# K of a cached-attention kernel loaded in four partition-interleaved transfers per pack instead of two

## The chip, the cores and the metric

The kernel runs on one core of a Trainium2 chip. The time is device microseconds from start to end of one execution. Each core has five engines that run their own instruction streams: TensorE (PE; its weight loads are shown as PEld), VectorE (DVE), ScalarE (ACT), GpSimd (POOL) and SyncE (SP, which here only issues DMAs). Sixteen DMA engines move data between HBM and the on-chip memory SBUF; matmul results go to PSUM.

## What is computed

Two independent attention blocks, A and B, of the same shapes, whose outputs are set side by side:

```python
B, Sq, D = 16, 64, 640          # x: [B, Sq, D]
H, Sk, Dh = 32, 512, 128        # k_cache, v_cache: [B, H, Sk, Dh]
q = (x @ wq).reshape(B, Sq, H, Dh).transpose(0, 2, 1, 3)
scores = einsum("bhqd,bhkd->bhqk", q, k_cache) * Dh ** -0.5
p = softmax(scores)
o = einsum("bhqk,bhkd->bhqd", p, v_cache)
block = o.transpose(0, 2, 1, 3).reshape(B, Sq, H * Dh) @ wo
out = concatenate([block_A, block_B], axis=-1)
```

All tensors are bfloat16. The caches are the bulk of the data: K and V of both blocks are 268 MB of the 295 MB that the profile shows moved.

## The kernel before

**Packs.** The work is cut into 128 packs. A pack is two batches times four heads: its K and its V are 1 MB each. Four consecutive packs (j = 0 to 3, 16 heads) share the same two batches, eight such groups make a phase (16 heads of all batches), and there are four phases (two blocks, two halves of the heads). The weights for a phase are loaded during the phase before.

**Steps of a pack n**, by the names in the code and the lines of the profile:
- LDK (`em_LDK`, L542 to L548): two DMAs of 512 KB, one for each batch b, of 64 rows of 8 KB (32 keys of 128 values). The rows of batch b go to every second partition, `kn_ring[b::2]`. The ring has 6 slots.
- LDV (`em_LDV`, L550 to L562): two DMAs of 512 KB, in rows of 4 KB for j = 0 to 2 and in two pieces of 2 KB for j = 3. The ring has 4 slots.
- QP (L598, PE) and QE (L604, ACT): project the queries and copy them out of PSUM.
- KT (`em_KT`, L608 to L613, DVE): two block transposes. Each takes 1024 elements per partition, read as 4-byte words (two bfloat16), and transposes them in blocks of 32 by 32 from `kn_ring` to `kt_ring`. The two batches lie interleaved on the partitions, so the 32 words of a transposed row belong to the two batches in turn; they are written apart by batch (`p c b k`), 16 words each.
- S (L622, PE): scores, 32 matmuls into four PSUM banks.
- EX (L641, ACT): exponentials with row sums; RC (L654, DVE): reciprocals; NM (L670, POOL): normalise.
- TR (L681, PE) transposes the probabilities, TE (L691, DVE) copies them out of PSUM in two instructions, PV (L705, PE) multiplies by V.
- OE, ZO (L713, L717, ACT) copy the result out and zero a bank; OP (L725, PE) multiplies by the output projection; after four packs OS (L735, L738, DVE) takes the sum, and for the second half of the heads ST (L744, ACT's queue) stores it.

**Order.** The order on every engine is written by a planner (`build_plan`). Each step has a time in units of packs (`Cfg.AT`), and each engine runs its steps in the order of those times. PE interleaves packs: PV(n-2), S(n), TR(n-1), OP(n-2), QP(n+1), PV(n-1). DVE: RC(n+1), KT(n+2) twice, TE(n) twice. SP issues all K, V, x and most weight loads in one fixed order, sorted by an issue time that the planner gives (K of a pack about 2.5 packs ahead of its V). Before each step the planner puts the semaphore waits that its data and buffers need: V of pack n waits for PV of pack n-4, K of pack n for the scores of pack n-6.

**Semaphores of loads.** K has one semaphore for each slot and batch, so KT waits for two. V has one for each slot, which both its DMAs raise; `wait_count` rounds a wait on it up to the full pair, and `Clocks.finish` joins what the two DMAs know.

Of the kernel before, what the change touches and what calls it, by code (L numbers as in the profile page):

```python
# [6 lines left out]
F32 = mybir.dt.float32  # L7
# [5 lines left out]
ENGINES = ("sp", "pe", "act", "dve", "pool")  # L13
SUM_MIN = 2.0 ** -40
SUM_MAX = 2.0 ** 40


class Cfg:
    NK = 6
# [11 lines left out]
    AT = dict(XT=-2.485, XE=-2.28, XC=-0.9, QP=-0.45, QE=-0.24, KT=(-1.24, -1.0), S=0,  # L31
              EX=(0.21, 0.32, 0.43, 0.54), RC=(0.53, 0.75), NM=(0.56, 0.69, 0.82, 0.95), NMZ=(0.54, 0.55, 0.56, 0.76), TR=1.2,
              TE=(1.26, 1.39), PV=1.75, OE=(2.0, 2.06), ZO=2.11, OP=2.31, OS=2.545, LDWO=2.6, ST=3.374, WP0=-1.75, WP1=-1.6)
# [22 lines left out]
def build_plan(dims, cfg, general):  # L56
# [7 lines left out]
    AT = cfg.AT  # L64
    ops = []
    loads = []
    at = {}

    def add(eng, kind, idx, ts, reads=(), writes=()):
        op = Op(eng, kind, idx, ts, reads, writes)  # L70
        ops.append(op)
        at[(kind, idx)] = op
        return op

    def add_output(n):
        g, j = n // NJ, n % NJ
        final = n >= 0 and dims["FINAL"](g // NBP)
        for b in range(2):
            tv = n + AT["PV"]
            op = add("sp", "LDV", (n, b), tv - 0.3, [], [("v" if n >= 0 else "absent", n % cfg.NV, b)])  # L80
            loads.append((n - cfg.NV + AT["PV"] + 0.2 if n >= 0 else -99.0, 3, op))
        if n > -2:
            add("pe", "TR", n, n + AT["TR"], [("pn", i) for i in range(4)] + [("ident",)], [("B", 4), ("B", 5)])
        for b in range(2):
            add("dve", "TE", (n, b), n + AT["TE"][b], [], [("B", 4 + b), ("pT", b)])
        add("pe", "PV", n, n + AT["PV"], [("pT", 0), ("pT", 1), ("v", n % cfg.NV, 0), ("v", n % cfg.NV, 1)],
            [("B", 4), ("B", 5), ("B67",)])
        add("act", "OE", (n, 1), n + AT["OE"][0], [], [("B67",), ("oT", 1)])
        add("act", "OE", (n, 0), n + AT["OE"][1], [], [("B", 4), ("B", 5), ("oT", 0)])
        add("act", "ZO", n, n + AT["ZO"], [("zeros",)], [("B67",)])  # L90
        add("pe", "OP", n, n + AT["OP"], [("oT", 0), ("oT", 1), ("wo", j)], [("B67",)])
        if j == NJ - 1:
            bp = g % NBP
            add("dve", "OS", g, n + AT["OS"], [("acc", bp)], [("B67",), ("out_sb",) if final else ("acc", bp)])
            if final:
                add("act", "ST", g, n + AT["ST"], [("out_sb",)], [("out_dram", g)])
# [4 lines left out]
    for g in range(N // NJ + 1):  # L101
# [5 lines left out]
        if dims["FIRST"](g // NBP):  # L107
            add("act", "XE", g, n0 + AT["XE"], [], [("SB", 0), ("xs", g % NBP)])
            op = add("sp", "LDX", g, txt - 0.5, [], [("xn", g % cfg.NXN)])
            loads.append((txt - 3.7 if g else -7.0, 0, op))  # L110
        add("pool", "XC", g, n0 + AT["XC"], [("xs", g % NBP)], [("xT", g % cfg.NX)])
    for ph in range(NPH):
        twp = [ph * PH + j + (AT["WP1"] if ph else AT["WP0"]) for j in range(NJ)]
        for kt in range(dims["KT"] if ph else 0):
            ready = twp[-1] - PH + 0.5 if ph > 1 else NJ - 1 + AT["WP0"] + 0.5
            op = add("sp", "LDWQ", (ph, kt), twp[0] - 0.5, [], [("ws", kt, j) for j in range(NJ)])
            loads.append((ready + 0.5 + 0.5 * kt if ph == 1 else ready + 2.0 + 0.14 * PH * kt, 1, op))
        for j in range(NJ):
# [3 lines left out]
            if not ph:  # L122
                op = add("sp", "LDWQ", (0, j), twp[j] - 0.5, [], [("ws", kt, j) for kt in range(dims["KT"])])
# [11 lines left out]
    for n in range(-2, N):  # L135
        add_output(n)
        if n < 0:
            continue
        g, j = n // NJ, n % NJ
        add("pe", "QP", n, n + AT["QP"], [("xT", g % cfg.NX), ("wqp", j)], [("SB", 1)])  # L140
        add("act", "QE", n, n + AT["QE"], [], [("SB", 1), ("qs", n % cfg.NQ)])
        for b in range(2):
            tk = n + AT["KT"][b]
            add("dve", "KT", (n, b), tk, [("kn", n % cfg.NK, 0), ("kn", n % cfg.NK, 1)], [("kt", n % cfg.NKT, b)])
            op = add("sp", "LDK", (n, b), n + AT["KT"][0] - 0.9, [], [("kn", n % cfg.NK, b)])
            loads.append((n - cfg.NV + AT["PV"] + 0.2 - cfg.KLEAD, 2, op))
        add("pe", "S", n, n + AT["S"], [("qs", n % cfg.NQ), ("kt", n % cfg.NKT, 0), ("kt", n % cfg.NKT, 1)],
            [("SB", i) for i in range(4)])
        for i in range(4):
            h = 4 * n + i  # L150
            te = n + AT["EX"][i]
            if general:
                add("dve", "MX", h, te - 0.002, [], [("SB", i), ("negmax", h % 4)])
            add("act", "EX", h, te, [("negmax", h % 4)] if general else [],
                [("SB", i), ("p", h % cfg.NP), ("rs", h)])
            add("pool" if n < N - 1 else "dve", "NM", h, n + (AT["NM"] if n < N - 1 else AT["NMZ"])[i], [("p", h % cfg.NP), ("recip", n % cfg.NR, i // 3)], [("pn", i)])
        for a in range(2):
            add("dve", "RC", (n, a), n + AT["RC"][a], [("rs", 4 * n + i) for i in ((0, 1, 2), (3,))[a]],
                [("recip", n % cfg.NR, a)])
# [156 lines left out]
class Clocks:  # L316
# [15 lines left out]
    def finish(self, eng, op):  # L332
        ck = self.clock[eng]
        self.val[op.sem] = self.val.get(op.sem, 0) + 1
        c2 = dict(ck)
        if op.dma:
            c2[op.sem] = op.count
        else:
            self.own[eng][op.sem] = op.count
            for s2, v2 in self.own[eng].items():  # L340
                if c2.get(s2, 0) < v2:
                    c2[s2] = v2
        if op.sem[0] == "d_v" and op.count % 2 == 0:
            for s2, v2 in self.snap[(op.sem, op.count - 1)].items():
                if c2.get(s2, 0) < v2:
                    c2[s2] = v2
        self.snap[(op.sem, op.count)] = c2


def wait_count(d):  # L350
    return d.count + d.count % 2 if d.sem[0] == "d_v" else d.count


def order_waits(progs, need, base):
    ks = Clocks(base)

    def visit(eng, op):
        want = {}
        for d in need[id(op)]:
            want[d.sem] = max(want.get(d.sem, 0), wait_count(d))  # L360
        if any(ks.val.get(s, 0) < v for s, v in want.items()):
            return False
        ck = ks.clock[eng]
        cand = [(s_, v_) for s_, v_ in want.items() if ck.get(s_, 0) < v_]
        keep = list(cand)
        for w in list(cand):
            for o in keep:
                if o != w and ks.snap[o].get(w[0], 0) >= w[1]:
                    keep.remove(w)
                    break  # L370
        op.waits = keep
        ks.learn(eng, keep)
        ks.finish(eng, op)
        return True

    run_order(progs, visit)
# [46 lines left out]
def mha_kernel(nc, blocks, out, cfg=None):  # L423
    cfg = cfg or Cfg()
# [4 lines left out]
    KT = D // 128  # L429
# [11 lines left out]
    for general in (False, True):  # L441
        dims = dict(NPH=NPH, NBP=NBP, NJ=NJ, KT=KT, FIRST=lambda ph: ph % NSUB == 0,
                    FINAL=lambda ph: ph % NSUB == NSUB - 1)
        plans.append(build_plan(dims, cfg, general))
    NK, NV, NKT, NX, NXN, NQ, NP, NR = (cfg.NK, cfg.NV, cfg.NKT, cfg.NX, cfg.NXN, cfg.NQ, cfg.NP, cfg.NR)

    with contextlib.ExitStack() as es:
        block = es.enter_context(nc.Block())

        def sb(name, shape, dt):  # L450
            return es.enter_context(nc.sbuf_tensor(name, shape, dt))
# [4 lines left out]
        kn_ring = sb("kn_ring", [128, NK, 2, 2048], BF16)  # L456
# [33 lines left out]
        def pack_info(n):  # L490
            g, j = n // NJ, n % NJ
            ph = g // NBP
            return ph // NSUB, g % NBP, j, ph % NSUB * HPH + 4 * j
# [46 lines left out]
            return ins, ins  # L540

        def em_LDK(e, op):  # L542
            n, b = op.idx
            blk, bp, j, h = pack_info(n)
            src = blocks[blk][1][2 * bp + b, h:h + 4].rearrange("h (p t) d -> (h p) (t d)", t=32)
            dst = kn_ring[b::2, n % NK].rearrange("p a c -> p (a c)")
            ins = e.dma_start(dst, src)  # L547
            return ins, ins  # L548

        def em_LDV(e, op):  # L550
# [57 lines left out]
        def em_KT(e, op):  # L608
            n, a = op.idx
            dst = kt_ring[:, n % NKT, 16 * a:16 * a + 16].rearrange("p t j b k two -> p (t j) b (k two)").bitcast(F32)  # L610
            ins = e.transpose(dst.rearrange("p c b k -> p c k b"),  # L611
                              kn_ring[:, n % NK, a, :].bitcast(F32).rearrange("p (c k b) -> p c k b", k=16, b=2))
            return ins, ins  # L613

        def em_S(e, op):
# [133 lines left out]
        def em_FL1(e, op):  # L749
# [3 lines left out]
            e.wait_ge(s_ch, 2)  # L753
            e.tensor_scalar(extreme[:, 2:3], extreme[:, 0:1], SUM_MAX, None, ALU.is_le).then_inc(s_ch, 1)
            e.tensor_scalar(extreme[:, 3:4], extreme[:, 1:2], SUM_MIN, None, ALU.is_ge).then_inc(s_ch, 1)
# [147 lines left out]
```

## Time and profile before

| | |
|---|---|
| median of 10 runs | 753.63 us (751.88 to 755.1) |
| the profiled execution | 754.1 us |
| its span, first to last instruction | 752.4 us |
| granted TensorE clock, mean | 0.981 |
| PE / DVE / ACT / POOL busy | 679.6 / 677.3 / 520.1 / 404.0 us |
| moved by DMA | 295.13 MB, mean 392 GB/s |
| DMA packets | 83421, of these 74736 on SP's queue |
| K load, issue to landing | median 12.6 us (A), 16.5 us (B) |
| V load, issue to landing | median 11.7 us (A), 13.8 us (B) |

A line of a group in the profile reads: line of the kernel, engine, operation, written tile <- read tiles, shapes, count | busy us, mean ns of one | idle time of the engine just before, and what ended it. The slice rows cut the span into 40 equal slices of 18.8 us; a digit is the busy share in tenths. A row of a stage gives, after its length, the busy time of PE, PEld, DVE, ACT and POOL with the number of instructions, then the granted clock, the busy share of the DMA engines and GB/s. A line of waits reads: engine and line that waited <- engine and line that ended the wait: us in total, times, longest us. "SPq" is the issuing queue of SP.

### The profile page before, as it was taken

The numbers are of one execution on the slowest core, as the hardware profiler recorded it, in microseconds if no ns is written. First come the engines' busy times: TensorE is split into PE (matmuls) and PEld (weight loads), VectorE is DVE, ScalarE is ACT, GpSimd is POOL, SyncE is SP. The second block draws the span as 40 slices with busy tenths as digits, with TensorE's granted clock in tenths as the row PEclk, the third lists the DMA queues.
The fourth block names the chain that finished last, engine by engine and source line by source line (L and its number), as shares of the span: only waits on it lengthen the run. The fifth ranks groups of instructions, "written<-read, shape, count | busy, mean of one in ns | idle before, by whom it ended". The sixth has DMA issues, their size and how long they took to land.

```text
span 752.4 us, 57490 instructions
## 1 busy us (share of the span) xinstructions
PE 679.6 (90%) x26518; PEld 530.2 (70%) x26518; DVE 677.3 (90%) x818; ACT 520.1 (69%) x1559; POOL 404.0 (54%) x580
## 2 busy tenths in 40 slices
PE   3669999999999999999988989999998899999995
PEld 2547777777777777777766777777776677777773
DVE  8549999999999999999978899999997899999983
ACT  1437777877777777777756777777776577777772
POOL 5424555464875454645674455455586455545450
PEclk9979999999999999999999999999999999999996
DMA  8999999999999999999999999999999999999950
GB/s 314 399 402 410 411 411 414 411 411 413 408 399 410 416 413 414 412 413 413 413 399 407 410 411 412 410 413 412 412 407 398 411 415 413 412 414 412 406 195 14
DMA packets 83421, 295.13 MB, mean 392 GB/s; under 512 B 9264, under 2 KB 24112, under 8 KB 66992
## 3 DMA queue, kind: packets, MB, share of 16 engines
q1 hardware_dynamic: 74736, 284.20, 94.5%
q10 hardware_dynamic: 8640, 10.49, 3.9%
q14 instruction: 36, 0.29, 0.1%
q8 instruction: 9, 0.15, 0.1%
HBM read 292.03 MB, written 2.62 MB: 392 GB/s over the span
## 4 chain that ended last, share of the span: by engine, by line
DVE 28%; PE 24%; DMA 16%; SPq 12%; POOL 9%; ACT 5%; issue 5%; ACTq 0%; DVEq 0%
DVE kt_ring L611 20%; DMA kn_ring<-in_B_k_cache_dram 11%; POOL pn_sb L670 8%; PE ps L725 6%; PE ps L705 6%; DVE pT_sb L691 6%; SPq L547 5%; PE ps L598 5%; DMA kn_ring<-in_A_k_cache_dram 5%; ACT p_ring L641 5%; PE ps L622 3%; PE ps L681 3%; SPq L560 3%; SPq L558 2%; DVE recip L654 1%
## 5 line engine op out<-in xcount | busy, mean ns | idle before, releaser
L670 POOL TENSOR_SCALAR pn_sb<-p_ring,recip 128x512 bf16<-128x512 bf16 x508 | 341.8, 692 | 318.0 <-DVE recip L654 318.0
L611 DVE STREAM_TRANSPOSE kt_ring<-kn_ring 128x1024 f32<-128x1024 f32 x256 | 478.6, 1947 | 25.2 <-DMA kn_ring<-in_B_k_cache_dram 21.1
L641 ACT ACTIVATE p_ring<-ps 128x512 bf16<-128x512 f32 x512 | 298.7, 598 | 19.0 <-PE ps L622 4.2
L691 DVE COPY pT_sb<-ps 128x1024 bf16<-128x1024 bf16 x258 | 163.3, 675 | 24.4 <-PE ps L681 24.4
L705 PE MATMUL ps<-pT_sb,v_ring 32*128 32x64 bf16 (+1 forms) x14528 | 158.7, 192 | 22.5 <-DVE pT_sb L691 5.9
L725 PE MATMUL ps<-wo_sb,oT_sb 128*128 128x320 bf16 x1040 | 167.6, 305 | 6.4 <-issue 5.4
L598 PE MATMUL ps<-xT_ring,wqp_sb 128*128 128x128 bf16 x2560 | 167.0, 221 | 5.5 <-POOL xT_ring L587 5.5
L705 PEld LDWEIGHTS ps<-pT_sb,v_ring 32*128 32x128 bf16 (+1 forms) x14528 | 144.2, 92 | 37.4 <-issue 28.6
L598 PEld LDWEIGHTS ps<-xT_ring,wqp_sb 128*128 128x128 bf16 x2560 | 158.4, 114 | 12.0 <-issue 5.7
L713 ACT ACTIVATE oT_sb<-ps 128x256 bf16<-128x256 f32 x260 | 85.6, 381 | 107.4 <-PE ps L705 107.4
L604 ACT ACTIVATE qs_ring<-ps 128x512 bf16<-128x512 f32 x128 | 76.5, 597 | 91.8 <-PE ps L598 91.8
L622 PE MATMUL ps<-kt_ring,qs_ring 32*64 32x512 bf16 x4096 | 139.4, 383 | 0.0
L681 PEld LDWEIGHTS ps<-ident,pn_sb 64*128 64x128 bf16 x4128 | 71.1, 95 | 86.6 <-ACT ps L717 59.5
L725 PEld LDWEIGHTS ps<-wo_sb,oT_sb 128*128 128x128 bf16 x1040 | 92.1, 99 | 44.7 <-issue 5.9
L681 PE MATMUL ps<-ident,pn_sb 64*128 64x64 bf16 x4128 | 84.4, 191 | 29.0 <-POOL pn_sb L670 21.8
L641 ACT ACTIVATION_READ_ACCUMULATOR p_ring<-ps 128x1 f32 x512 | 106.0, 207 | 0.0
L622 PEld LDWEIGHTS ps<-kt_ring,qs_ring 32*64 32x64 bf16 x4096 | 53.3, 103 | 28.8 <-issue 1.0
L654 DVE RECIPROCAL recip<-rowsum 128x3 f32<-128x3 f32 (+1 forms) x256 | 39.4, 160 | 13.6 <-ACT p_ring L641 11.2
L717 ACT ACTIVATE ps<-zeros 128x256 f32<-128x256 bf16 x130 | 51.3, 395 | 0.0
L570 POOL COPY wqp_sb<-ws_sb 128x1280 bf16<-128x1280 bf16 x32 | 39.2, 1254 | 7.3 <-DMA ws_sb<-in_A_wq_dram 7.3
L587 POOL COPY xT_ring<-xs_sb 128x640 bf16<-128x640 bf16 x32 | 22.9, 716 | 3.6 <-PE ps L598 3.6
L577 PE MATMUL ps<-ident,xn_ring 128*128 128x128 bf16 x165 | 15.1, 224 | 3.6 <-DMA xn_ring<-in_A_x_dram 3.6
(26 smaller groups left out, 66.2 us busy)
## 6 DMA issues: line engine op xcount, KB each, us to landing
kn_ring<-in_A_k_cache_dram SPq DMA_DIRECT2D x128, 512.0 KB, 12.6
v_ring<-in_A_v_cache_dram SPq DMA_DIRECT2D x128, 512.0 KB, 11.7
kn_ring<-in_B_k_cache_dram SPq DMA_DIRECT2D x128, 512.0 KB, 16.5
v_ring<-in_B_v_cache_dram SPq DMA_DIRECT2D x128, 512.0 KB, 13.8
ws_sb<-in_B_wq_dram SPq DMA_DIRECT2D x10, 512.0 KB, 17.0
wo_sb<-in_B_wo_dram ACTq DMA_DIRECT2D x8, 640.0 KB, 15.3
ws_sb<-in_A_wq_dram SPq DMA_DIRECT2D x4, 640.0 KB, 9.7
wo_sb<-in_A_wo_dram SPq DMA_DIRECT2D x4, 640.0 KB, 13.8
```

Of the source, the lines that this page charges most:

```text
L598: last = e.matmul(ps[:, 1, f * 128:(f + 1) * 128], w[:, kt, f, :], xT_ring[:, xs, kt, :], start=(kt == 0), stop=(kt == KT - 1))
L604: ins = e.activation(qs_ring[:, op.idx % NQ].rearrange("p f b q -> p (f b q)"), ps[:, 1, :], ACTF.Copy, scale=scale)
L611: ins = e.transpose(dst.rearrange("p c b k -> p c k b"), kn_ring[:, n % NK, a, :].bitcast(F32).rearrange("p (c k b) -> p c k b", k=16, b=2))
L622: last = e.matmul(ps[64 * b:64 * b + 64, i, :], qs_ring[rows, n % NQ, f, b, :], kt_ring[rows, n % NKT, :, f // 2, b, :, f % 2], start=(f = ...
L641: ins = e.activation(dst, src, ACTF.Exp, scale=1.0, accum_out=rowsum[:, h:h + 1])
L670: ins = e.tensor_scalar(dst, src, recip[:, h // 4 % NR, i:i + 1], 1.0, ALU.mult, ALU.mult)
L681: last = e.transpose(pt_bank(b)[:, 64 * c:64 * c + 64], pn_sb[rows, c, :], ident[rows, rows], tile_position=(64 * b, 0))
L691: ins = e.tensor_copy(pT_sb[:, b].rearrange("p t q -> p (t q)"), pt_bank(b))
L705: last = e.matmul(ps[:, 4 + i, 64 * b:64 * b + 64], v_ring[rows, n % NV, b, c, :], pT_sb[rows, b, c, :], start=(t == 0 and i < 2), stop=(t ...
L713: ins = e.activation(oT_sb[:, 2 * a:2 * a + 2, :], o_ps[:, 2 * a:2 * a + 2, :], ACTF.Copy)
L717: ins = e.activation(z_ps, zeros[:, :].rearrange("p (s c) -> p s c", s=2), ACTF.Copy)
L725: last = e.matmul(out_ps[:, s, :], oT_sb[:, i, :], wo_sb[:, 4 * j + i, s * NH0:(s + 1) * NH0], start=(j == 0 and i == 0), stop=(j == NJ - ...
```

## The change

K of a pack comes by four DMAs of 256 KB instead of two of 512 KB. The rows stay 8 KB. Of batch b, the even rows (l = 0) and the odd rows (l = 1) are loaded by separate DMAs, each of 32 rows, to every fourth partition: `kn_ring[2 * b + l::4]`. So the partitions carry the batches in pairs (b0, b0, b1, b1, ...) where they carried them in turn (b0, b1, b0, b1, ...), and a transposed row of 32 words has two neighbouring words of a batch in a row. KT reads as before, in order; it writes `p c h b l`, where l, the innermost, steps to the neighbouring word. What `kt_ring` holds in the end, and every step after KT, are unchanged.

The four DMAs raise one semaphore per slot, and KT waits for that one at its full count; `PARTS` generalises for K (four) what was written for V (two).

```diff
+PARTS = dict(d_v=2, d_k=4)
...
+        for i in range(4):
+            op = add("sp", "LDK", (n, i), n + AT["KT"][0] - 0.9, [], [("kn", n % cfg.NK)])
+            loads.append((n - cfg.NV + AT["PV"] + 0.2 - cfg.KLEAD, 2, op))
         for b in range(2):
             tk = n + AT["KT"][b]
-            add("dve", "KT", (n, b), tk, [("kn", n % cfg.NK, 0), ("kn", n % cfg.NK, 1)], [("kt", n % cfg.NKT, b)])
-            op = add("sp", "LDK", (n, b), n + AT["KT"][0] - 0.9, [], [("kn", n % cfg.NK, b)])
-            loads.append((n - cfg.NV + AT["PV"] + 0.2 - cfg.KLEAD, 2, op))
+            add("dve", "KT", (n, b), tk, [("kn", n % cfg.NK)], [("kt", n % cfg.NKT, b)])
...
-        if op.sem[0] == "d_v" and op.count % 2 == 0:
-            for s2, v2 in self.snap[(op.sem, op.count - 1)].items():
+        part = PARTS.get(op.sem[0], 1)
+        for k in range(op.count - 1, (op.count - 1) // part * part, -1):
+            for s2, v2 in self.snap[(op.sem, k)].items():
...
 def wait_count(d):
-    return d.count + d.count % 2 if d.sem[0] == "d_v" else d.count
+    part = PARTS.get(d.sem[0], 1)
+    return -(-d.count // part) * part
...
         def em_LDK(e, op):
-            n, b = op.idx
+            n, b, l = op.idx[0], op.idx[1] // 2, op.idx[1] % 2
             blk, bp, j, h = pack_info(n)
-            src = blocks[blk][1][2 * bp + b, h:h + 4].rearrange("h (p t) d -> (h p) (t d)", t=32)
-            dst = kn_ring[b::2, n % NK].rearrange("p a c -> p (a c)")
-            ins = e.dma_start(dst, src)
+            src = blocks[blk][1][2 * bp + b, h:h + 4].rearrange("h (p l t) d -> l (h p) (t d)", l=2, t=32)[l]
+            ins = e.dma_start(kn_ring[2 * b + l::4, n % NK].rearrange("p a c -> p (a c)"), src)
             return ins, ins
...
         def em_KT(e, op):
             n, a = op.idx
             dst = kt_ring[:, n % NKT, 16 * a:16 * a + 16].rearrange("p t j b k two -> p (t j) b (k two)").bitcast(F32)
-            ins = e.transpose(dst.rearrange("p c b k -> p c k b"),
-                              kn_ring[:, n % NK, a, :].bitcast(F32).rearrange("p (c k b) -> p c k b", k=16, b=2))
+            src = kn_ring[:, n % NK, a, :].bitcast(F32).rearrange("p (c h b l) -> p c h b l", h=8, b=2, l=2)
+            ins = e.transpose(dst.rearrange("p c b (h l) -> p c h b l", h=8, l=2), src)
             return ins, ins
```

## The prediction

> **What bounds the kernel now.** I read the busy row of the DMA engines first, then the idle time of each engine by stage, then who waits for whom, then single packs from the landing times.
>
> The page:
>
> ```profile
> PE   3669999999999999999988989999998899999995
> DVE  8549999999999999999978899999997899999983
> DMA  8999999999999999999999999999999999999950
> GB/s 314 399 402 410 411 411 414 411 411 413 408 399 410 416 413 414 412 413 413 413 399 407 410 411 412 410 413 412 412 407 398 411 415 413 412 414 412 406 195 14
> L611 DVE STREAM_TRANSPOSE kt_ring<-kn_ring 128x1024 f32<-128x1024 f32 x256 | 478.6, 1947 | 25.2 <-DMA kn_ring<-in_B_k_cache_dram 21.1
> ```
>
> The DMA engines are at 9 tenths from the second slice to about 715 us, and 398 to 416 GB/s hardly changes, whatever the other engines do. The stages in numbers (engine times, then clock, DMA share, GB/s):
>
> ```profile
> 60.00:145.00 85.00, 82.18 (x3288) 64.53 (x3286) 82.92 (x101) 65.82 (x198) 45.70 (x68) 1.00 1.03 411
> 515.00:600.00 85.00, 76.27 (x3008) 59.97 (x3014) 75.99 (x94) 58.12 (x176) 51.32 (x71) 1.00 1.03 408
> 645.00:730.00 85.00, 82.64 (x3290) 64.97 (x3288) 82.86 (x102) 63.60 (x194) 45.70 (x68) 1.00 0.95 381
> ```
>
> In two kinds of stage, one with DVE 97% busy and one with 89%, the DMA share is the same 1.03 (above 1 because records of neighbouring packets overlap). So the queue never runs dry before 715 us, and as SP issues in one fixed order, the moment at which each K and V lands is set by the DMA engines alone. The waits say the same (the first two lines from SP's own queue, the third from 600 to 730 us):
>
> ```profile
> SPq L558 <- PE ps L705: 141.9, 61, 6.8
> SPq L560 <- PE ps L705: 73.9, 30, 4.1
> PE ps L681 <- POOL pn_sb L670: 2.0, 6, 0.4
> ```
>
> SP waits for V slots, yet the queue behind it holds some 15 us of transfers (K takes a median 15.8 us from issue to landing). And PE hardly waits for anybody: 2.4 us of the 85 from 645 us on. Three engines are level: DVE, PE and DMA.
>
> What computing adds to the transfers is the end. From landing times and first PV matmuls: K of pack 102 lands at 592.8 us and its transpose starts at 592.9; from there computing falls behind, K of pack 123 waits 1.9 us for its transpose (702.7 to 704.6) and K of pack 127 2.7 us (723.1 to 725.8). V of pack 123 lands at 715.7 us and is used at 720.4, V of 127 at 730.8 and is used at 741.2. After that come 11.2 us of projection, sum and store in which nothing is transposed.
>
> **The transpose.** Price per element from DVE's contiguous 4-byte writes in this trace:
>
> ```profile
> L735 DVE COPY acc<-ps 128x640 f32<-128x640 f32 x17 | 13.5, 797 | 0.1
> L509 DVE MEMSET v_ring<- 128x4096 uint32 x1 | 3.5, 3472 | 1.7 <-PEq L888 1.7
> L517 DVE MEMSET wo_sb<- 128x2560 uint32 x1 | 2.2, 2192 | 0.5 <-DMA kn_ring<-in_A_k_cache_dram 0.5
> ```
>
> (3472 - 2192) / (4096 - 2560) = 0.833 ns each; the copy is 640 x 0.833 = 533 plus 264 fixed. A transpose of 1024 elements at two such steps each is 1707 + 240 = 1947, exactly its row. So each element now takes two steps, and its write lies 64 bytes from the last. If a run of two removes the second step: 853 + 240 = 1.09 us. If the second step belongs to transposing 4-byte words at all: 1.95 us, no gain. No row shows an 8-byte run. I take 1.1 us, since every contiguous write in the trace goes at one step and the fixed part agrees; both ends stay in the range. A pair then takes 3.75 - 2 x 0.85 = 2.05 us, 1.7 us less (bounds 0 and 1.7).
>
> [...]
>
> **Where that lies.** 256 x 0.85 = 218 us leave DVE, but nearly all lies beside a saturated DMA queue and a PE with 3% idle. On the path stand two pieces, both at the end. (a) KT(n+2) stands ahead of TE(n) in DVE's order, so when K lands late, pair, TE and PV follow each other; 1.7 us shorter. (b) The lag gathered after pack 102: DVE, at 5.31 us a pack, is slower than K lands (597.9 for pack 103, 702.7 for 123: 5.24 a pack). With DVE at about 3.6 us, PE decides: 5.31 less its 2.8% idle is 5.16, quicker than landings. So the lag of 1.9 us at pack 123 goes. Together 3.6 us; V allows 4.7 there. Late next is the landing itself; after pack 123 PE's pace has the four last packs, which took 20.8 us. Bounds: 0 (no faster transpose) to 4.4 (2.7 + 1.7 at pack 127).
>
> **The transfers.** K has 4 x 128 = 512 DMAs where it had 256, each of 256 KB; bytes and the 8 KB rows stay. By the trace's packet records a packet takes 51 ns for 1024 bytes, 57 for 1280, 87 for 2048, 163 for 4096, 315 for 8192: about 11 ns + 38 ns a KB, whether rows follow each other in HBM (V of j = 0 to 2) or lie apart (V of j = 3, weights). So I price K's packet, now every second 8 KB row, at the same 315. Added are 256 x 16 semaphore packets of 9.5 ns, 16 engines in parallel: 2.4 us; records overlap by some 3.9 ns a packet (0.026 of 20 us over 135 packets an engine), which makes it 1.4. I take 1.9, all on the path, since the queue is never dry. Bounds: 0 if the packet hides in others, and upwards the price of K by V's packets, 2 x 163 = 326: 16384 / 16 x 11 ns = 11.3 us.
>
> [...]
>
> **SP.** A K issue takes 0.48 to 0.60 us unblocked, a V pair 0.82. Per pack SP has 2 x 0.54 + 0.82 = 1.9 us now, 4 x 0.54 + 0.82 = 3.0 then, of 5.2. K's four are contiguous in SP's order; behind them wait the next V pair (which waits for PV anyway), x and weights. At nothing: the 15 us of queue hides it, and uncovered it is 1.1 us a pack. In the first 6 us, where the DMA engines are not full, up to 0.5 us; included in the 1.9. DVE drops one of two waits ahead of KT; no cost either way.
>
> **Sum.** On the profiled execution: 754.1 (span 752.4 and 1.7 around it) - 3.6 + 1.9 = 752.4. It stands 0.5 above the median of the ten, 753.63, so I forecast **751.9**: -0.23%. About 0.2% (1.5 us) is what a measurement of this kernel can tell from no change; the forecast lies at that edge.
>
> **Rivals.**
> 1. Both halves kinder: added packets hide (0) and the lag goes to 4.4: 749.2. For it: overlapping records. Against: semaphore packets do have time of their own.
> 2. The transpose is not faster, or by half: gain 0 to 1.8, cost 1.9: 753.7 to 755.5. For it: two steps can be the price of a 4-byte transpose. Then the change doesn't do what it says.
> 3. Slower by one mechanism: K's packets. Every ns on a K packet is 1024 packets an engine = 1.0 us, on the path everywhere, as the queue has no gap. From 1.7 ns (0.5%) on it eats the net gain; by V's price it is 751.9 + 11.3 = 763.2. For it: rows that an engine reads no longer follow each other, and two are written where four were. Against: the straight line through five sizes, apart or not.
>
> **How the numbers follow.** Forecast case 0.55 (751 to 753: faster 0.35, same 0.20), rival 1 0.12 (faster), rival 2 0.18 (same 0.10, slower 0.08), rival 3 0.15 (slower 0.14, same 0.01). Faster 0.47, same 0.31, slower 0.22. The range takes in rivals 1 and 2 and the lower third of rival 3: 749.2 to 756.5, leaving out about 0.12. Cases of both signs are in it; the forecast case's own range is 751 to 753.
>
> **What would show it.** Right: the transpose at about 1.1 us; DVE near 60% busy; POOL still beside; DMA share still 1.03 to 715 us; 4096 more 4-byte packets; K waiting under 0.5 us for its transpose at pack 123; the wait of KT for K grown far beyond 25 us; K's packets at 315 ns. Wrong: K's packets above 317 ns; gaps in the DMA row (then transfers were not the bound or SP starves them); transpose at 1.9; PE idle grown before 715 us in stages where K lands in time.

## The result and the profile after

The changed kernel takes 749.74 us in the median of 8 runs (748.72 to 750.12), the kernel before 753.35 us in 28 runs. The ratio is 0.9952 with a 95% interval of 0.9942 to 0.9961: 3.6 us less (2.9 to 4.4). The profiled execution took 748.7 us, its span 747.0.

The same rows of the changed kernel's page (slices of 18.7 us):

```profile
PE   4669999999999999999988999999898899999994
DVE  7437777777777677686756776777676687877773
DMA  8999999999999999999999999999999999999970
GB/s 319 399 402 410 412 411 414 411 411 412 407 399 414 412 413 412 412 413 413 412 398 407 411 413 412 412 411 410 412 409 401 409 414 412 413 413 412 412 303 16
L617 DVE STREAM_TRANSPOSE kt_ring<-kn_ring 128x1024 f32<-128x1024 f32 x256 | 302.9, 1222 | 110.5 <-DMA kn_ring<-in_B_k_cache_dram 78.3
```

DVE falls from 9 to 7 and 6 tenths. The DMA row and the GB/s row are what they were. The 303 in place of 195 near the end is no faster drain: that slice begins at 709.7 us in the changed kernel and at 714.8 before. A transpose takes 1222 ns for 1947, and it now waits 110.5 us in all for K where it waited 25.2.

The same three stages:

```profile
60.00:145.00 85.00, 83.90 (x3369) 66.32 (x3368) 65.93 (x105) 67.17 (x201) 47.28 (x71) 1.00 1.03 411
515.00:600.00 85.00, 76.53 (x3045) 60.24 (x3043) 58.64 (x91) 58.17 (x176) 51.37 (x71) 1.00 1.03 408
645.00:730.00 85.00, 83.96 (x3340) 65.43 (x3327) 65.17 (x100) 64.18 (x196) 46.72 (x70) 1.00 0.95 381
```

The DMA share is 1.03 and the rates are 411 and 408 GB/s, to the digit as before. From 645 us on PE is busy 83.96 of 85 us instead of 82.64. SP's own waits in the changed kernel:

```profile
SPq L563 <- PE ps L710: 48.9, 28, 4.3
SPq L565 <- PE ps L710: 17.8, 10, 4.1
```

They fall from 216 to 67 us. Not all of that is PV freeing the V slots earlier, as SP now also has twice as many K loads to issue: in the two experiments below with one half of the change each, these waits are 128 us (the transpose alone) and 110 (the loads alone). The engines' waits over the whole span have a line that is new in size:

```profile
DVE pT_sb L696 <- PE ps L686: 67.3, 58, 10.4
```

TE waited 24.4 us, 8 times, for TR before. Two of these eight are the last two packs, 126 and 127, in the kernel before:

```profile
734.32 1.29 DVE L691 COPY pT_sb<-ps 128x1024 bf16<-128x1024 bf16 x2 [3.39 <-PE ps L681]
739.73 1.29 DVE L691 COPY pT_sb<-ps 128x1024 bf16<-128x1024 bf16 x2 [2.66 <-PE ps L681]
```

And the waits of the changed kernel from 600 to 730 us:

```profile
DVE kt_ring L617 <- DMA kn_ring<-in_B_k_cache_dram: 12.9, 23, 0.9
```

In this stage no transpose waited for K before; now K's landing holds it up in 23 of some 25 packs. The transposes of packs 123 and 127 start as K lands, after VectorE has been idle:

```profile
701.91 2.37 DVE L617 STREAM_TRANSPOSE kt_ring<-kn_ring 128x1024 f32<-128x1024 f32 x2 [0.55 <-DMA kn_ring<-in_B_k_cache_dram]
722.59 2.37 DVE L617 STREAM_TRANSPOSE kt_ring<-kn_ring 128x1024 f32<-128x1024 f32 x2 [0.38 <-DMA kn_ring<-in_B_k_cache_dram]
```

Before, K of pack 127 landed at 723.1 us and its transposes started at 725.8.

In the profiled execution of before the closing stage, from the first PV matmul of pack 127 to the end, took 11.2 us (741.2 to 752.4); in the changed kernel 9.3 (737.7 to 747.0), and 9.6 in three of the experiments below, one of which has the old transposes. From 730 us on the granted clock was 0.74 in the kernel before:

```profile
730.00:752.00 22.00, 12.85 (x460) 8.98 (x458) 7.28 (x21) 6.57 (x22) 2.69 (x4) 0.74 0.04 13
```

In the changed kernel it is 0.92 (from 730 us to its end). So I count some 1.6 of the 5.4 us between the two profiled executions as no part of the change; the medians' 3.6 is what is to be explained, and PV of pack 127, 3.5 us earlier, is where it stands.

### The profile page after: what moved, and what is told of

Its sections match the earlier page's. It is cut to its first block, busy times and chain, and to the rows that moved or that the text cites. A ratio compares the mean times of both kernels' runs of the same rounds, so it can differ in the third digit from the quotient of the medians.

```text
span 747.0 us, 57618 instructions
## 1 busy us (share of the span) xinstructions
PE 679.7 (91%) x26518; PEld 530.5 (71%) x26518; DVE 526.0 (70%) x818; ACT 518.9 (69%) x1559; POOL 404.0 (54%) x580
## 4 chain that ended last, share of the span: by engine, by line
PE 39%; SPq 28%; DMA 12%; POOL 6%; ACT 5%; DVE 5%; issue 5%; ACTq 0%; DVEq 0%
SPq L552 19%; PE ps L710 10%; PE ps L730 9%; PE ps L603 8%; DMA kn_ring<-in_B_k_cache_dram 8%; POOL pn_sb L675 6%; PE ps L627 5%; SPq L563 5%; PE ps L686 5%; SPq L565 3%; ACT p_ring L646 3%; DMA v_ring<-in_B_v_cache_dram 2%; DVE kt_ring L617 2%; DMA kn_ring<-in_A_k_cache_dram 2%; ACT oT_sb L718 2%
## 5 line engine op out<-in xcount | busy, mean ns | idle before, releaser
L617 DVE STREAM_TRANSPOSE kt_ring<-kn_ring 128x1024 f32<-128x1024 f32 x256 | 302.9, 1222 | 110.5 <-DMA kn_ring<-in_B_k_cache_dram 78.3
L696 DVE COPY pT_sb<-ps 128x1024 bf16<-128x1024 bf16 x258 | 164.4, 678 | 68.0 <-PE ps L686 67.3
L710 PE MATMUL ps<-pT_sb,v_ring 32*128 32x64 bf16 (+1 forms) x14528 | 161.8, 192 | 26.9 <-DVE pT_sb L696 9.1
L582 PE MATMUL ps<-ident,xn_ring 128*128 128x128 bf16 x165 | 14.9, 222 | 4.4 <-DMA xn_ring<-in_A_x_dram 3.5
```

The source lines that it names most:

```text
L617: ins = e.transpose(dst.rearrange("p c b (h l) -> p c h b l", h=8, l=2), src)
L696: ins = e.tensor_copy(pT_sb[:, b].rearrange("p t q -> p (t q)"), pt_bank(b))
L710: last = e.matmul(ps[:, 4 + i, 64 * b:64 * b + 64], v_ring[rows, n % NV, b, c, :], pT_sb[rows, b, c, :], start=(t == 0 and i < 2), stop=(t ...
```

## The experiments

Each is run against the kernel before on the same chip. Kernels whose K packets were slow scatter by some per cent from run to run (1090 to 1159 us for one of them), so of these only the packet time and the order of size are used. Packet times are means of the trace's DMA records.

**The load half alone.** Four loads, but to the partitions of the old layout; old transpose.

```diff
-            ins = e.dma_start(kn_ring[2 * b + l::4, n % NK].rearrange("p a c -> p (a c)"), src)
+            ins = e.dma_start(kn_ring[b + 2 * l::4, n % NK].rearrange("p a c -> p (a c)"), src)
...
+            ins = e.transpose(dst.rearrange("p c b k -> p c k b"),
+                              kn_ring[:, n % NK, a, :].bitcast(F32).rearrange("p (c k b) -> p c k b", k=16, b=2))
```

> Only the load half of the change: four DMAs of 256 KB a pack (rows l of batch b to partitions b + 2l, every fourth), partition layout and transpose as before. Theory A (the transfers' queue is always full, so 256 added DMAs cost their semaphore packets): 1.4 to 2.4 us slower than before, ratio 1.002 to 1.003. Theory B (the packets hide, the loads are free): ratio 1.000, within 0.7 us. Theory C (finer loads help by themselves, as K and V landed 0.7 us earlier in the changed kernel's trace): 0.7 us or more faster, ratio 0.999 or less. In all three the transpose stays at 1.95 us.

Measured: 753.76 us, ratio 1.0008 (0.9997 to 1.002), so 0.6 us slower, between 0.2 faster and 1.5 slower. Theory A's lower end, 1.4, lies just inside the interval, B fits better, and C is excluded at its 0.7 us. The transpose takes 1938 ns, as the old one does. The trace shows where part of the added packets' time stays: 4096 more packets of 9.2 ns, but K's packets take 314.7 ns instead of 315.4, which over 1024 of them on each DMA engine is 0.7 us. In every kernel below whose four loads run at full speed they take 314.7 to 315.1, in both kernels with two loads 315.4 to 315.7. From 20 to 700 us 278.7 MB were moved, 278.8 before.

**The transpose half alone.** Two loads of 512 KB with the new layout: load l carries the rows of both batches in turn.

```diff
-            src = blocks[blk][1][2 * bp + b, h:h + 4].rearrange("h (p l t) d -> l (h p) (t d)", l=2, t=32)[l]
-            ins = e.dma_start(kn_ring[2 * b + l::4, n % NK].rearrange("p a c -> p (a c)"), src)
+            src = blocks[blk][1][2 * bp:2 * bp + 2, h:h + 4].rearrange("b h (p l t) d -> l (h p) b (t d)", l=2, t=32)[l]
+            ins = e.dma_start(kn_ring[l::2, n % NK].rearrange("p a c -> p (a c)"), src)
```

> Only the transpose half of the change: partitions carry the batches in pairs and the transpose writes runs of two, but K comes by two DMAs of 512 KB as before (one for each l, each with rows of both batches in turn, to every second partition). Theory A: 1.4 to 2.4 us faster than the changed kernel, ratio to before 0.992 to 0.9935. Theory B: same as the changed kernel, 0.9952. Theory C: slower than the changed kernel by 0.7 us, 0.996. The transpose at 1.22 us, as in the changed kernel, in all three.

Measured: 748.81 us, ratio 0.9948 (0.9935 to 0.9962), transpose 1222 ns. The whole gain comes with the transpose: 3.9 us (2.9 to 4.9). That is theory B. Against the changed kernel's 0.9952 the difference is 0.3 us, less than either interval: two or four loads can't be told apart by their time. K of pack 123 lands at 703.5 us and its transpose starts at 703.6; before it waited from 702.7 to 704.6. The lag is gone, as in the changed kernel.

**Vector work put back, behind TE.** Changed kernel, three reductions of a constant tile after TE in each pack.

```diff
+        def em_PAD(e, op):
+            first = last = None
+            for i in range(3):
+                last = e.tensor_reduce(pad[:, i:i + 1], zeros[:, :], AX.X, ALU.max)
+                first = first or last
+            return first, last
...
+        add("dve", "PAD", n, n + AT["TE"][1] + 0.001, [("zeros",)], [])
```

> The changed kernel with about 1.3 us of idle work added on VectorE in each pack, behind the copies of TE (three reductions of a constant tile), so that VectorE is again about as long as before (5.2 to 5.3 us a pack), while K's landing to TE stays shorter by 1.45 us. If the gain is both the shorter path from K's landing and the lag that VectorE's pace gathered after pack 102: about half of the gain is lost, ratio 0.997 to 0.998. If it is the path alone: 0.9952 stays. If it is the pace alone: 0.999 to 1.000.

Measured: 813.2 us, ratio 1.0792 (1.0773 to 1.0812), far from all three. The place was wrong, and the time line of VectorE says why:

```profile
650.81 1.29 DVE L698 COPY pT_sb<-ps 128x1024 bf16<-128x1024 bf16 x2 [1.29 <-PE ps L688]
652.01 1.06 DVE L704 TENSOR_REDUCE pad<-zeros 128x1 f32<-128x256 bf16 x3
652.99 0.21 DVE L661 RECIPROCAL recip<-rowsum 128x3 f32<-128x3 f32 x2
653.12 2.35 DVE L619 STREAM_TRANSPOSE kt_ring<-kn_ring 128x1024 f32<-128x1024 f32 x2
656.77 1.29 DVE L698 COPY pT_sb<-ps 128x1024 bf16<-128x1024 bf16 x2 [1.29 <-PE ps L688]
```

VectorE idles 1.29 us before each TE although it has 1.06 us of idle work in the pack. The work delays RC, RC releases NM on POOL (2.7 us), NM releases TR, TR releases TE, and TE stands ahead of the next work: a closed loop of 656.77 - 650.81 = 5.96 us. (The profile puts most of TR's waits down to EX on ACT, which ends within some 0.1 us of NM here. In the kernel before TR starts while EX runs, so I take NM to be what TR waits for.) This says nothing on the two pieces of the gain, but it points to a loop TE, RC, NM, TR that has little slack at 5.2 us a pack.

**Vector work put back, ahead of the transposes.** Four such reductions after RC and before KT, so that they neither delay RC nor stand between KT and TE.

```diff
-        add("dve", "PAD", n, n + AT["TE"][1] + 0.001, [("zeros",)], [])
+        add("dve", "PAD", n, n + AT["KT"][0] - 0.005, [("zeros",)], [])
```

> The changed kernel with about 1.4 us of idle work (four reductions of a constant tile) added on VectorE in each pack ahead of the two transposes, where VectorE otherwise waits for K when K is late. VectorE is then about as long as before in a pack, but K's landing to TE stays 1.4 us shorter. If the gain is both the path from K's landing and the lag of VectorE's pace: about half of the gain lost, ratio 0.997 to 0.998. Path alone: 0.9952. Pace alone: 0.999 to 1.000.

Measured: 753.55 us, ratio 1.0012 (1.0003 to 1.0021): the whole gain is lost, which is nearest to the expectation for the pace alone, and the transpose is still the fast one. VectorE is back where it was, in the stage from 645 us on and in the waits of its transposes on the page:

```profile
645.00:730.00 85.00, 82.63 (x3276) 64.73 (x3274) 82.21 (x164) 62.43 (x191) 45.70 (x68) 1.00 0.96 383
```

```profile
L619 DVE STREAM_TRANSPOSE kt_ring<-kn_ring 128x1024 f32<-128x1024 f32 x256 | 302.7, 1221 | 26.3 <-DMA kn_ring<-in_B_k_cache_dram 21.2
```

82.21 of 85 us busy, and 26.3 us of waiting for K as before (25.2). Its transposes start 5.4 us apart (pack 115 at 663.1, 119 at 684.7; before 5.3: 662.2, 683.4), and K of pack 122 waits 2.4 us for its transpose. So VectorE's pace over the last 25 packs decides. The added work is a little more than what the transposes gave up, so that it also covers a small gain on the path; the traces suggest such a piece: from the start of KT(123) to PV(123) it is 14.7 us here, 14.9 with two loads and 15.2 in the changed kernel, for 15.8 before.

**Runs of four words.** Batches interleaved by fours of partitions, four loads of 32 rows to every fourth partition.

```diff
-            ins = e.dma_start(kn_ring[2 * b + l::4, n % NK].rearrange("p a c -> p (a c)"), src)
+            src = blocks[blk][1][2 * bp:2 * bp + 2, h:h + 4].rearrange("b h (p l t) d -> l (h p) b (t d)", l=4, t=32)[l]
+            ins = e.dma_start(kn_ring[l::4, n % NK].rearrange("p a c -> p (a c)"), src)
...
-            ins = e.transpose(dst.rearrange("p c b (h l) -> p c h b l", h=8, l=2), src)
+            ins = e.transpose(dst.rearrange("p c b (h l) -> p c h b l", h=4, l=4), src)
```

> The changed kernel with the batches interleaved by fours of partitions, so that the transpose writes runs of four 4-byte words (16 bytes); four loads of 32 rows, each with rows of both batches in turn, to every fourth partition. If two words a run already give one step an element: transpose stays at 1.21 to 1.22 us, time the same as the changed kernel, ratio 0.995. If runs of two still pay for changing place: transpose at about 1.09 us (853 + 240), and the time at most 0.3 us less, since the end goes by K's landing.

Measured: the transpose takes 1223 ns, so runs of two already give all that runs of four would. But the kernel takes 1134 us, half as long again: K's packets go from 315 to 492 ns and V's of 4 KB from 163 to 247. Neither expectation foresaw that; the next experiments ask where it comes from.

**Eight loads.** Changed kernel, eight loads of 16 rows to every eighth partition.

```diff
+            n, b, l, m = op.idx[0], op.idx[1] // 4, op.idx[1] // 2 % 2, op.idx[1] % 2
+            src = blocks[blk][1][2 * bp + b, h:h + 4].rearrange("h (p m l t) d -> m l (h p) (t d)", m=2, l=2, t=32)[m, l]
+            ins = e.dma_start(kn_ring[4 * m + 2 * b + l::8, n % NK].rearrange("p a c -> p (a c)"), src)
```

> The changed kernel with its K loads halved again: eight DMAs of 128 KB a pack, 16 rows each, to every eighth partition; 512 DMAs more than the changed kernel, transpose the same. Theory A: 2.9 to 4.9 us slower than the changed kernel, ratio to before 0.999 to 1.002. Theory B: the same as the changed kernel, 0.995 to 0.996. Theory D (SP's issue becomes the bound: 8 x 0.55 us + 0.82 = 5.2 us a pack, as long as a pack): DMA share falls below 1.0 in the middle of the run, and over 5 us slower.

Measured: 1124 us (1090 to 1159). None of the three: the DMA engines are busy in every slice, yet move 256 GB/s, and K's packets take 507 ns, V's 245.

```profile
DMA  9999999999999999999999999999999999999991
DMA packets 95715, 295.24 MB, mean 256 GB/s; under 512 B 21552, under 2 KB 36400, under 8 KB 79280
```

From 300 to 600 us their share is 1.03, so they don't run dry and theory D isn't it either.

**Four loads by halves of the partitions.**

```diff
+            n, l, hh = op.idx[0], op.idx[1] % 2, op.idx[1] // 2
+            src = blocks[blk][1][2 * bp:2 * bp + 2, h + 2 * hh:h + 2 * hh + 2]
+            src = src.rearrange("b h (p l t) d -> l (h p) b (t d)", l=2, t=32)[l]
+            ins = e.dma_start(kn_ring[64 * hh + l:64 * hh + 64:2, n % NK].rearrange("p a c -> p (a c)"), src)
```

> The changed kernel, still four K loads of 32 rows a pack, same layout and transpose, but each load fills every second partition of one half of the partitions (0 to 63 or 64 to 127) instead of every fourth of all 128. It asks why K's packets went from 315 to 506 ns with eight loads to every eighth partition. Theory P (what counts is how many separate groups of partitions a load reaches: the eight loads reached only half of the groups of four; a half of the partitions does too): K's packets well above 315 ns, toward 500, and the kernel tens of percent slower. Theory Q (what counts is the number of loads or the rows per load: 16 rows, one a DMA engine): K's packets at 315 ns and the same time as the changed kernel, ratio 0.995.

Measured: 1142 us, K's packets 532 ns, as theory P has it; four loads can be as slow as eight, so theory Q falls. But this kernel changes two things. Call the first dimension of a load's source, `(h p)` in the edits, its outer rows: the changed kernel has 32 of them, this one 16 of two rows each, and the eight loads 16 of one. So it doesn't tell the partitions from the division of the source.

**Source and destination apart.** Three kernels that differ in one side of K's loads. The source moved, to 32 rows that lie 32 KB apart:

```diff
+            src = blocks[blk][1][2 * bp + b, h // 8 * 8:h // 8 * 8 + 8]
+            src = src.rearrange("h (p l t) d -> l (h p) (t d)", l=4, t=32)[2 * (j % 2) + l]
```

The destination moved, to every second partition of one half:

```diff
+            ins = e.dma_start(kn_ring[64 * b + l:64 * b + 64:2, n % NK].rearrange("p a c -> p (a c)"), src)
```

Eight loads to every eighth partition, with the source rows of each together:

```diff
+            src = blocks[blk][1][2 * bp + b, h + m].rearrange("(p t) d -> p (t d)", t=32)
+            ins = e.dma_start(kn_ring[4 * b + m::8, n % NK].rearrange("p a c -> p (a c)"), src)
```

> The changed kernel with only the source of its K loads moved: 32 rows of 8 KB that lie 32 KB apart in HBM (over eight heads) where the change has them 16 KB apart (over four); destinations, sizes and number of loads as in the changed kernel. K's rows reach other partitions than they should, so the scores are of permuted keys and heads; every row is still read once. Theory H (K's packets go to 500 ns when the DMA engines read HBM at too regular a distance): K's packets near 500 ns, time 1.4 times and more. Theory S (what counts is which partitions a load writes): 315 ns and the time of the changed kernel, 0.995. Theory G (what counts is that each DMA engine gets only one outer row of the source): 315 ns, 0.995.

> The changed kernel with only the destination of its K loads moved: each writes every second partition of one half (batch 0 to partitions 0 to 63, batch 1 to 64 to 127), sources as in the changed kernel (32 rows, 16 KB apart, one batch). The layout isn't the one that the transpose expects, so the scores are of permuted keys and batches. Theory S: K's packets near 500 ns, 1.4 times and more. Theories H and G: 315 ns, 0.995.

> The eight loads of 16 rows to every eighth partition, as in the kernel with eight loads, but each load's 16 rows follow one another in HBM (one head's 128 KB); the keys reach other partitions than they should, so the scores are of permuted keys and heads. Theory H: K's packets back at 315 ns, and the time that 512 added loads cost by their semaphore packets or less, ratio 0.995 to 0.999. Theories S and G: K's packets at 500 ns, 1.4 times and more.

Measured: with the source moved 750.41 us, ratio 0.9965 (0.9952 to 0.9977), K's packets 314.7 ns; with the destination moved 1250 us, 546 ns; with eight loads and rows together 1230 us, 552 ns. The distance of the rows in HBM, 16 or 32 KB, makes no difference, so theory H falls. The second kernel differs from the changed one in nothing but the partitions that a load writes, so these decide there: S holds, and G is not the only cause, as this kernel has 32 outer rows. For the eight loads S and G expect the same.

**The runs of four again: destination as in the change, source in pairs of rows.**

```diff
+            src = blocks[blk][1][2 * bp + b, h:h + 4]
+            src = src.rearrange("(x h) (p l t) d -> l (h p) x (t d)", x=2, l=2, t=32)[l]
+            ins = e.dma_start(kn_ring[2 * b + l::4, n % NK].rearrange("p a c -> p (a c)"), src)
```

> It asks why the loads with runs of four were slow although they wrote the same partitions as the changed kernel's (every fourth). The changed kernel with the source of each K load in two dimensions: 16 rows 16 KB apart times two pairs of heads 256 KB apart, all of one batch; destination every fourth partition, as in the changed kernel. [...] Keys reach other partitions than they should, so the scores are of permuted keys and heads. [...] If the jump from one batch to the other in the source made the runs of four slow: K's packets at 315 ns and ratio 0.995.

Measured: 1110 us, K's packets 477 ns. The jump between batches is not the cause. With 32 partitions written as in the change, 16 outer rows of two are slow and 32 outer rows are fast; the kernel with two loads, 32 outer rows of two, is fast as well. So the division of the source counts beside the partitions: all five kernels with 16 outer rows are slow (477 to 552 ns), whichever partitions they write. Only the kernel with the destination moved shows the partitions by themselves (546 ns); in the eight loads and the halves either cause would do, and no run separates the two there.

By partitions, the four kernels whose loads write one half of them, or every eighth, took 507 to 552 ns, and three of these have 16 outer rows as well; the two that write every fourth from 16 outer rows of two took 477 and 492; those that write every fourth or every second from 32 or 64 outer rows took 314.7 to 315.7. Why these partitions and these sources are slow was not shown. That an engine gets one row of sixteen, as theories Q and G have it, was my assumption: the trace doesn't tell which engine moved which row.

**All of V in rows of 4 KB.**

```diff
-    WIDE = (0, 1, 2)
+    WIDE = (0, 1, 2, 3)
```

> The changed kernel with V of every fourth pack (j = 3) also loaded in rows of 4 KB (and its probabilities laid out and multiplied as for the other packs), so that 16384 packets of 2 KB become 8192 of 4 KB. It takes transfer time away and adds a little to TensorE: PV of such a pack about 1.15 us for 1.05. If the landing sets the end, as the prediction has it now: 512 x (87.2 - 3.9) less 256 x (162.5 - 3.9) over 16 engines is 0.13 us a pack of 32, 4.1 us less, ratio to before 0.990. If TensorE sets it: 32 x 0.1 = 3 us slower than the changed kernel, 0.999. Both at once: 0.993 to 0.996.

Measured: 1378 us, ratio 1.833 (1.826 to 1.841). It didn't test what it was meant to. Its PE program, in which four packs form one loop, has grown (28630 matmuls executed for 26518), and the instruction queue (packets, MB, share of 16 engines) has grown too; the line of the changed kernel's page is first, then that of this one:

```profile
q8 instruction: 9, 0.15, 0.1%
```

```profile
q8 instruction: 290, 4.75, 1.5%
```

290 fetches of instructions, of 16 KB each, for 9; and long waits of PE are put down to "issue", that is, to nothing that the profile shows:

```profile
PEld ps L603 <- issue: 211.5, 32, 7.8
PE ps L603 <- issue: 194.5, 31, 7.5
```

I take it from these that the grown loop fetches its code again while it runs; no size between was tried. Whether V in fewer and larger packets would help is left open.

No kernel was clearly faster than the changed one. The one with two loads is the simpler form of the change, at the same time.

## Why the prediction was right, and where its sum was not

The time fell by 0.48%, within the stated range, in the direction that was given the most weight, but by twice the 0.23% of the forecast. Step by step (the profiled executions are compared up to PV of pack 127, as said above):

- **What bounds.** Right. DMA share and rates are unchanged, and 1.4 us of VectorE a pack taken away (478.6 to 302.9 us busy) gave 3.6 us of 753. In the changed kernel and with two loads K's last transposes start as K lands.
- **The transpose.** 1.22 us for 1.1, so VectorE is busy 526 of 747 us, 70%, and not near 60%. A transpose lost 725 ns, 0.71 ns an element, less than the step of 0.833 that I had from MEMSET rows. Either the fixed part grew by 129 ns, or the step is another: a VectorE row of one element, the reciprocal, takes 156 ns, and with that as the fixed part the new transpose goes at 1.04 ns an element and the old one at 1.75. With one length of transpose the two can't be told apart. That runs of four take 1223 ns shows that two words a run are enough here; why they are was not shown.
- **Piece (b), the lag of VectorE's pace, 1.9 us.** Right in kind: loading VectorE again takes the whole gain away, with the fast transpose in place. It was taken at pack 123; at pack 127, the last, the lag that went was 2.7.
- **Piece (a), the path from K's landing, 1.7 us.** Too large. From KT(123) to PV(123) only 0.6 us went in the changed kernel (15.8 to 15.2; 0.9 and 1.1 in two experiments), and from KT(127) to PV(127) 0.3 (15.4 to 15.1). The waits say what takes its place: TE now waits for TR, 67.3 us in 58 times. The pair ends earlier, but TE needs what PE does in its own order. At the last two packs TE waited for TR in the kernel before, too, 3.39 and 2.66 us; I had followed KT and TE on VectorE and not asked what else TE waits for.
- **The transfers, 1.9 us on the path.** This is the term that most made the forecast too small. The load half alone costs 0.6 us (-0.2 to 1.5). The packets of 9.2 ns are there, 4096 of them, but a packet's record was no measure here of what the queue loses: K's packets became 0.7 ns shorter with four loads (314.7 for 315.4).
- **The sum.** By the changed kernel's trace at pack 127: 2.7 us of lag, 0.5 by which K lands earlier (722.6 for 723.1, not explained) and 0.3 of path make the 3.5 us by which PV(127) starts earlier; the medians say 3.6 (2.9 to 4.4). That pieces (a) and (b) came to 3.6 together was partly luck: one was too large and the other too small. A single trace is not sure to a microsecond: with two loads KT(127) starts at 724.2, only 1.6 us earlier than before, but the execution profiled there took 750.76 us, the longest of its six.
- **Rival 3, K's packets.** It didn't happen, but it was nearer than I thought, and its reason was wrong. I weighed whether rows lie apart in HBM, where the straight line through five sizes held, and it holds (32 KB apart: 314.7 ns). What I named second, two rows written where four were (an estimate: a load's 32 and 64 rows over 16 engines), points at the writing side, but the number of rows is not what counts: with 32 rows a load K's packets take 315 ns in the changed kernel, 546 when they go to one half of the partitions, and 477 when the same partitions are filled from 16 outer rows. The kernel then takes 1.5 to 1.7 times the time. That the change's every fourth partition and its 32 outer rows make a good load was luck of the forecast, not shown by the trace of before.

## What to carry to other kernels

Where the DMA engines are full in every slice and issue order is fixed, as here (share 1.03), a faster engine was worth only the lag that it had gathered at the end: 176 us less work on VectorE gave 3.6 us, of which 2.7 were the lag at pack 127. Read it as the wait between the last landings and their first use, and before adding a second piece ask what else its next step waits for. When a load is cut up or its layout changed, look first at which partitions each piece writes and how its source is divided, and check the packet time of the same size (here 315 ns, or 477 to 552), not the number of transfers (256 more cost 0.6 us). Idle work put back at one place of an engine is a clean test of a pace (753.55 us, ahead of the transposes), if it is kept out of the loops that pass through that engine (813.2 us, behind TE).

## What was not expected of the hardware

- VectorE's transpose of 1024 4-byte words a partition took 1947 ns when it wrote them 64 bytes apart, 1222 with runs of two words, and no less with runs of four (1223).
- The same 8 KB rows, in the same number, take 315 ns a packet or 477 to 552, by the partitions that one load writes and by how its source is divided; the packets of other loads in the queue slow down with them (V's of 4 KB from 163 to between 229 and 274 ns).
- 256 more loads in a full queue cost 0.6 us (-0.2 to 1.5).
- With 2112 more matmuls over the run (28630 for 26518), all in PE's loop, came 281 more instruction fetches of 16 KB and 1.8 times the time.
